# Weights converted quarter by quarter, and six blocks passed over each quarter

## The chip, the cores and the metric

The kernel runs on one core of a Trainium2 chip. The metric is the time of one execution on the device in microseconds (us). In the text TensorE is also PE, VectorE DVE, ScalarE ACT, GpSimd POOL and SyncE SP; PEld is TensorE's weight load.

## The reference

Two stages. A recurrent attention (RWKV-5) over 4 batches, 8 heads, 768 steps and head size 48, then a dense layer with a nonlinear step, on 3072 tokens of 384 numbers:

```
for t in range(S):
    cur = einsum('bhd,bhe->bhde', u * k[t], v[t])
    y[t] = einsum('bhd,bhde->bhe', r[t], state + cur)
    state = w * state + einsum('bhd,bhe->bhde', k[t], v[t])
x = y as (4*768, 384)
h = x @ w_in            # w_in  384 x 2048
g = h - tanh(h)
out = g @ w_out         # w_out 2048 x 384
```

The attention's inputs are 4-byte floats. The two weight matrices reach the kernel as 8-byte floats, which no engine computes with: the kernel loads them as pairs of 4-byte words and builds a 4-byte float from the bits.

## The kernel before, in words

**Attention.** The work is cut into 24 units. A unit takes 64 steps of two batches, all heads, so 128 tokens. It loads r, k and v (six transfers of 96 KB on SP's queue), scales k by powers of the decay (`kw`), turns r and k on TensorE into the PSUM tile `x_ps`, scales the turned r (`rT`) on VectorE and copies the turned k (`kT`) on ScalarE, multiplies them into `x_ps` again, applies the causal mask to the result with a predicated copy on VectorE (L390, into `at`), and multiplies `at` by v, and r by the running state, into the PSUM tile `yk_ps`. ScalarE copies the result into `xt`, six small transfers move the rest of the rows (`xt<-rest`, L410), and VectorE and GpSimd bring the state up to date (L416, L419). `rk` (L370, L371) and `du` (L374) give the diagonal, which GpSimd spreads into `at` (L376). Both PSUM tiles have one buffer, and each of the two batch pairs has one state, so a unit needs the one two before it.

**Dense.** Two units make a block, 12 blocks in all. A block goes over its 16 hidden tiles of 128 in 8 pairs (f, f+1). For a pair, twelve matmul instructions write `h` (L151); ScalarE makes s = h squared, th = tanh(h) and two squares q1, q2; GpSimd makes the mask `small` of the places where s is below 0.25 (L166); VectorE makes g = h - th, and, where h is small, replaces it by a polynomial `cube` (L167 to L171). Two pairs later eight matmul instructions add g times w_out into two PSUM tiles `o` (L177), which hold the sums of the whole block; then ScalarE copies them and SP writes them out (L190, L194).

**Weights.** `weight_steps` cuts them into 28 chunks, of 128 x 512 for w_in and 128 x 384 for w_out. Each is loaded on ScalarE's queue into a staging tile `st`, with two buffers, and converted in one step on ScalarE (L113), five on VectorE (L114 to L118) and two on GpSimd (L119, L120).

**Order.** Each engine takes its instructions in the order of the program. Python generators yield pieces of work, and `weave` interleaves them in proportion; a scheduler then orders the instructions by readiness, within what the buffers allow. `drive` weaves block 0 with the first half of the chunks, block 1 with the second half, and from then on the dense work of block j with the attention of block j+2. A dense block needs all 28 chunks, up to the last of its pairs.

Next to `near` stands `anywhere`, a second way for other decay values. It is in the program behind a branch on `flag` and isn't executed with these inputs.

Of the kernel before, what the change touches and what calls it, by code (L numbers as in the profile page):

```python
# [1 line left out]

# [6 lines left out]
F32 = mybir.dt.float32  # L9
# [10 lines left out]
SMALL = 0.25  # L20
# [13 lines left out]
L = 2  # L34

# [51 lines left out]
def weight_steps(nc, stage, w_in_sb, w_out_sb, moe_w_in, moe_w_out, d):  # L87
    V, A, G = nc.vector, nc.scalar, nc.gpsimd
    w_out_v = moe_w_out.rearrange("(ko ki) f -> ki ko f", ki=128)

    def weight(dst, pieces, dtype, cols):

        if dtype == F32:
            def g():
                for to, src in pieces:
                    nc.scalar.dma_start(out=dst[to], in_=src)

            return g


        assert dtype == I64

        def f():
            st = stage.tile([128, 512], I64, name="st", tag="st")[:, :cols]
            for to, src in pieces:
                nc.scalar.dma_start(out=st[to], in_=src)
            words = st.bitcast(U32).rearrange("p (n t) -> p n t", t=2)
            lo, hi = words[:, :, 0], words[:, :, 1]
            lo_f = st.bitcast(F32).rearrange("p (n t) -> p n t", t=2)[:, :, 0]
            part = stage.tile([128, 512], U32, name="part", tag="part")[:, :cols]  # L110
            part_f = part.bitcast(F32)
            bits = dst.bitcast(U32)
            A.activation(lo_f, lo, AF.Copy, scale=2.0**-52)  # L113
            V.tensor_scalar(part, hi, 3, 0x3FFFFFFF, ALU.logical_shift_left, ALU.bitwise_and)  # L114
            V.scalar_tensor_tensor(bits, hi, 0xC0000000, part, ALU.bitwise_and, ALU.bitwise_or)  # L115
            V.tensor_scalar(hi, hi, 20, 0x7FF, ALU.logical_shift_right, ALU.bitwise_and)  # L116
            V.scalar_tensor_tensor(dst, hi, 897.0, dst, ALU.is_ge, ALU.mult)  # L117
            V.tensor_scalar(part, bits, 0xFF800000, None, ALU.bitwise_and)  # L118
            G.tensor_tensor(part_f, part_f, lo_f, ALU.mult)  # L119
            G.tensor_tensor(dst, dst, part_f, ALU.add)  # L120

        return f

    weights = []
    for q in range(d.DFF // 512):
        sl = slice(q * 512, (q + 1) * 512)
        for ko in range(d.NK):
            pieces = []
            for to, kk, row, n in row_blocks(d):
                if kk is None:  # L130
                    row += ko * 2 * d.D
                if kk in (None, ko):
                    pieces.append((slice(to, to + n), moe_w_in[row : row + n, sl]))
            weights.append(weight(w_in_sb[:, ko, sl], pieces, moe_w_in.dtype, 512))
        for f in range(4 * q, 4 * q + 4):
            weights.append(weight(w_out_sb[:, f, :], [(slice(0, 128), w_out_v[:, f, :])], moe_w_out.dtype, d.DM))
    return weights


def make_dense(nc, work, gpool, ps_d, w_in_sb, w_out_sb, m1b, m2b, out, d, rows):  # L140

    V, A, T, G = nc.vector, nc.scalar, nc.tensor, nc.gpsimd

    def dense(j, xt):
        outs = [ps_d.tile([128, d.DM], F32, name=f"o{i}", tag=f"o{i}", bufs=1) for i in range(L)]

        def first(f):
            h = ps_d.tile([128, 2, d.NT], F32, name="h", tag="h")
            for z in range(2):
                for kk in range(d.NK):  # L150
                    T.matmul(h[:, z], w_in_sb[:, kk, (f + z) * 128 : (f + z + 1) * 128],  # L151
# [545 lines left out]
```

## Time and profile before

| | |
|---|---|
| Median of 3 runs | 727.84 us (726.28 to 729.05) |
| Profiled execution, its own time | 725.77 us |
| Span in the profile, first to last instruction | 724.0 us |
| Busy: PE, DVE, ACT, POOL | 620.9, 492.4, 279.5, 352.6 us |
| Mean granted TensorE clock | 0.946 |
| Transferred | 33.8 MB, mean 47 GB/s |

The profile's page divides the span into 40 slices of 18.1 us and gives each engine's busy share in tenths. A view by stage gives busy time in chosen stretches. Groups of instructions have a line, an engine, an operation, shapes and a count, then busy time in us and mean in ns, then the idle time just before them and what ended it. Timeline rows start with the start and the length in us. Waits are written "who <- whom: us in total, times, longest". PE's share of busy time is an average over two stages of different kinds, so the stretches are read apart.

### The profile page before, as it was taken

The numbers are of one execution on the slowest core, as the hardware profiler recorded it, in microseconds if no ns is written. First come the engines' busy times: TensorE is split into PE (matmuls) and PEld (weight loads), VectorE is DVE, ScalarE is ACT, GpSimd is POOL, SyncE is SP. The second block draws the span as 40 slices with busy tenths as digits, with TensorE's granted clock in tenths as the row PEclk, the third lists the DMA queues.
The fourth block names the chain that finished last, engine by engine and source line by source line (L and its number), as shares of the span: only waits on it lengthen the run. The fifth ranks groups of instructions, "written<-read, shape, count | busy, mean of one in ns | idle before, by whom it ended". The sixth has DMA issues, their size and how long they took to land.

```text
span 724.0 us, 13305 instructions
## 1 busy us (share of the span) xinstructions
PE 620.9 (86%) x5060; PEld 453.2 (63%) x5060; DVE 492.4 (68%) x739; ACT 279.5 (39%) x510; POOL 352.6 (49%) x289
## 2 busy tenths in 40 slices
PE   1462473657999999999999999999999999999996
PEld 0351452435776777777677777767777777777773
DVE  7764788989875664864865766748648656576563
ACT  1110413223443543444444434435435444354442
POOL 4775876758654543634545445436345243133231
PEclk9997586767999999999999999999999999999999
DMA  9457243422210211202102102112120010000001
GB/s 145 99 127 138 68 101 90 108 80 74 51 36 11 55 29 41 41 15 58 26 13 58 36 10 58 30 31 42 24 47 15 1 27 3 4 23 1 23 1 27
DMA packets 89722, 33.80 MB, mean 47 GB/s; under 512 B 80561, under 2 KB 86066, under 8 KB 89650
## 3 DMA queue, kind: packets, MB, share of 16 engines
q1 hardware_dynamic: 85042, 20.28, 14.9%
q10 hardware_dynamic: 4608, 12.59, 6.3%
q8 instruction: 42, 0.69, 0.4%
q14 instruction: 30, 0.25, 0.1%
HBM read 26.94 MB, written 4.72 MB: 44 GB/s over the span
## 4 chain that ended last, share of the span: by engine, by line
PE 68%; DVE 12%; DMA 8%; POOL 6%; issue 4%; SPq 1%; ACT 0%; ACTq 0%; DVEq 0%; POOLq 0%
PE o L177 33%; PE h L151 27%; PE yk_ps L348 4%; DMA st<-in_moe_w_out_dram 4%; DMA rt<-in_r_dram 3%; POOL part L119 3%; PE x_ps L363 2%; POOL rk L370 2%; POOL rk L371 2%; DVE st L116 1%; DVE part L114 1%; DVE w_in_sb L117 1%; DVE part L118 1%; DVE w_in_sb L115 1%; DVE cube L170 1%
## 5 line engine op out<-in xcount | busy, mean ns | idle before, releaser
L151 PE MATMUL h<-xt,w_in_sb 128*128 128x256 f32 x1152 | 276.4, 389 | 20.6 <-POOL w_in_sb L120 20.5
L177 PE MATMUL o<-w_out_sb,g 128*128 128x384 f32 x768 | 270.0, 498 | 11.8 <-DVE g L171 11.8
L166 POOL TENSOR_SCALAR small<-s 128x512 f32<-128x512 f32 x96 | 146.1, 1523 | 258.0 <-ACT s L162 249.7
L151 PEld LDWEIGHTS h<-xt,w_in_sb 128*128 128x128 f32 x1152 | 217.1, 194 | 59.8 <-POOL w_in_sb L120 22.9
L177 PEld LDWEIGHTS o<-w_out_sb,g 128*128 128x128 f32 x768 | 146.8, 194 | 102.4 <-issue 11.6
L167 DVE SCALAR_TENSOR_TENSOR cube<-s,h 128x512 f32<-128x512 f32 x96 | 65.7, 685 | 122.6 <-ACT th L163 122.4
L162 ACT ACTIVATE s<-h 128x512 f32<-128x512 f32 x96 | 57.3, 597 | 190.7 <-PE h L151 87.1
L170 DVE SCALAR_TENSOR_TENSOR cube<-q,cube 128x512 f32<-128x512 f32 x96 | 79.2, 825 | 7.6
L171 DVE COPY_PREDICATED g<-small,cube 128x512 f32<-128x512 int32 x96 | 78.5, 818 | 5.6
L169 DVE SCALAR_TENSOR_TENSOR cube<-q,cube 128x512 f32<-128x512 f32 x96 | 74.8, 779 | 0.0
L164 ACT ACTIVATE q<-s,m1b 128x512 f32<-128x512 f32 x96 | 69.3, 722 | 9.9 <-POOL part L119 9.9
L165 ACT ACTIVATE q<-s,m2b 128x512 f32<-128x512 f32 x96 | 69.0, 719 | 0.0
L168 DVE TENSOR_TENSOR g<-h,th 128x512 f32<-128x512 f32 x96 | 65.5, 682 | 0.0
L163 ACT ACTIVATE th<-h 128x512 f32<-128x512 f32 x96 | 56.8, 592 | 2.7 <-POOL part L119 2.7
L119 POOL TENSOR_TENSOR part<-part,st 128x384 f32<-128x384 f32 (+1 forms) x28 | 35.9, 1280 | 39.6 <-DVE part L118 22.8
L348 PE MATMUL yk_ps<-rT,state 48*64 48x64 f32 x704 | 27.7, 234 | 24.3 <-DVE state L416 19.3
L113 ACT ACTIVATE st<-st 128x384 f32<-128x384 uint32 (+1 forms) x28 | 17.1, 610 | 73.3 <-POOL part L119 34.5
L348 PEld LDWEIGHTS yk_ps<-rT,state 48*64 48x64 f32 x704 | 24.6, 146 | 33.1 <-issue 28.2
L376 POOL TENSOR_TENSOR at<-same,du 128x512 f32<-128x512 f32 x24 | 30.9, 1286 | 23.9 <-PE yk_ps L348 21.4
L365 DVE TENSOR_TENSOR rT<-x_ps,w_up 128x512 f32<-128x512 f32 x24 | 16.4, 685 | 29.3 <-PE x_ps L363 29.3
L374 DVE TENSOR_REDUCE du<-rk 128x8 f32<-128x384 f32 x24 | 13.2, 550 | 33.3 <-POOL rk L371 33.3
L370 POOL TENSOR_TENSOR rk<-rt,kt 128x384 f32<-128x384 f32 x24 | 26.6, 1109 | 16.5 <-DMA rt<-in_r_dram 9.5
(71 smaller groups left out, 459.8 us busy)
## 6 DMA issues: line engine op xcount, KB each, us to landing
st<-in_moe_w_out_dram ACTq DMA_DIRECT2D x16, 384.0 KB, 3.0
st<-in_moe_w_in_dram ACTq DMA_DIRECT2D x24, 192.0 KB, 3.3
rt<-in_r_dram SPq DMA_DIRECT2D x48, 96.0 KB, 3.1
kt<-in_k_dram SPq DMA_DIRECT2D x48, 96.0 KB, 3.0
vt<-in_v_dram SPq DMA_DIRECT2D x48, 96.0 KB, 2.8
out_dram<-o SPq DMA_DIRECT2D x48, 96.0 KB, 2.2
xt<-rest SPq DMA_DIRECT2D x144, 8.0 KB, 1.8
st<-in_moe_w_in_dram ACTq DMA_DIRECT2D x24, 64.0 KB, 3.3
```

Source lines behind the costliest of these rows:

```text
L119: G.tensor_tensor(part_f, part_f, lo_f, ALU.mult)
L151: T.matmul(h[:, z], w_in_sb[:, kk, (f + z) * 128 : (f + z + 1) * 128], xt[:, kk].rearrange("p b t -> p (b t)"), start=kk == 0, stop=kk == ...
L164: A.activation(q1, s, AF.Square, bias=m1b)
L165: A.activation(q2, s, AF.Square, bias=m2b)
L166: G.tensor_scalar(small, s, SMALL, None, ALU.is_lt)
L167: V.scalar_tensor_tensor(cube, s, C4, hf, ALU.mult, ALU.mult)
L168: V.tensor_tensor(gf, hf, th, ALU.subtract)
L169: V.scalar_tensor_tensor(cube, q1, K1, cube, ALU.add, ALU.mult)
L170: V.scalar_tensor_tensor(cube, q2, K2, cube, ALU.add, ALU.mult)
L171: V.copy_predicated(gf, small.bitcast(I32), cube)
L177: T.matmul(outs[i], g[:, z, i * C : (i + 1) * C], w_out_sb[:, f + z, :], start=f + z == 0, stop=f + z == d.NF - 1)
L348: tc.keep_in_program_order(T.matmul(*args, skip_group_check=True, **how))
```

## The change

- **Order of the dense work.** `FIRST = 6`. The hidden tiles are cut into four quarters of four (two pairs). After the attention of blocks 0 and 1, blocks 0 to 5 are taken over quarter 0, one after the other, then over quarter 1, 2 and 3. Beside quarter 0 run the twelve units of blocks 2 to 7. Blocks 6 to 11 run as before, each whole, with the attention of block j+2 beside it.
- **Partial sums.** After a quarter a block's sums leave PSUM: by a ScalarE copy into `part` for quarter 0 (L209), and by a VectorE addition for the others (L203). There are 12 `part` tiles and 8 `xt` tiles.
- **Weights.** Eight pieces, alternately a quarter of w_in and a quarter of w_out, each 128 x 1536. A piece is loaded by eight transfers (w_in) or one (w_out), into one of two staging buffers; the load of piece n+2 is issued after piece n is converted. Conversion has two steps on ScalarE (L142, L144) and five on VectorE (L141, L143, L146, L147, L149), none on GpSimd.
- **Attention of blocks 0 to 7.** `kw`, and the two products of `rk`, are on VectorE; the diagonal is spread by eight ScalarE instructions on 64 columns (L428). From block 8 on they are on GpSimd as before. The small `xt<-rest` transfers are made once per block, not per unit.
- **Mask.** `small` is made on ScalarE as relu(0.25 - s) (L181); a place counts where that is not zero. `cube` shares the buffer of `th`.
- The check of the decay uses a column sum on TensorE, and some set-up tiles share buffers.

The core of the diff:

```diff
+FIRST = 6
-            G.tensor_tensor(part_f, part_f, lo_f, ALU.mult)
-            G.tensor_tensor(dst, dst, part_f, ALU.add)
+        V.tensor_scalar(power, hi, 0x7FF00000, None, ALU.bitwise_and)
+        A.activation(power, power, AF.Relu, scale=8.0, bias=self.bias)
+        V.tensor_scalar(bits, hi, 0xFFFFF, 0x100000, ALU.bitwise_and, ALU.bitwise_or)
+        A.activation(lo_f, lo, AF.Copy, scale=2.0**-52)
+        yield
+        V.scalar_tensor_tensor(dst, bits, 2.0**-20, lo_f, ALU.mult, ALU.add)
+        V.scalar_tensor_tensor(power, hi, 0x80000000, power, ALU.bitwise_and, ALU.bitwise_or)
+        yield
+        V.tensor_tensor(dst, dst, power.bitcast(F32), ALU.mult)
...
-            G.tensor_scalar(small, s, SMALL, None, ALU.is_lt)
+        A.activation(small, s, AF.Relu, bias=smallb, scale=-1.0)
...
+        begun, whole = fs[0] > 0, fs[1] == d.NF
+        for i in range(L):
+            if begun:
+                o = sums.pop((j, i)) if whole else sums[j, i]
+                V.tensor_tensor(o, outs[i], o, ALU.add)
+            else:
...
+                    o = sums[j, i] = work.tile([128, d.DM], F32, name="part", tag="part", bufs=L * FIRST)
+                A.copy(o, outs[i])
...
+        weave(blocks([0, 1]), pieces([0, 1]))
+        after()
+        part = d.NF // 4
+        for q in range(4):
+            fs = (q * part, (q + 1) * part)
+            js = range(FIRST)
+            streams = [(chain.from_iterable(dense(j, xts[j], fs) for j in js), FIRST * part // 2)]
+            if q == 0:
+                streams.append(blocks(range(2, FIRST + 2)))
+            if q < 3:
+                streams.append(pieces([2 * q + 2, 2 * q + 3]))
+            weave(*streams)
...
+        early = n < L * (FIRST + 2)
+        E = V if early else G
+        E.tensor_tensor(kw[:, :, :D], kt, w_down, ALU.mult)
...
+        for h in range(H if early else 0):
+            A.mul(at[:, h % 2, h // 2], same, du[:, h : h + 1])
```

What the change moves, at the three places on which the prediction rests. First VectorE right after the set-up (`same`), where the first unit and the first weights meet. Before (`part` and `st` belong to the weights, `du`, `rT` and `at` to attention):

```order
L300 TENSOR_TENSOR same<-ident 128x64
L114 TENSOR_SCALAR part<-st 128x512
L115 SCALAR_TENSOR_TENSOR w_in_sb<-st,part 128x512
L374 TENSOR_REDUCE du<-rk 128x8
L116 TENSOR_SCALAR st<-st 128x512
L117 SCALAR_TENSOR_TENSOR w_in_sb<-st,w_in_sb 128x512
L118 TENSOR_SCALAR part<-w_in_sb 128x512
L365 TENSOR_TENSOR rT<-x_ps,w_up 128x512
```

Now, with the two first pieces and the third unit's `rk` ahead of the first unit's `kw` and `rT`:

```order
L141 TENSOR_SCALAR power<-st 128x1536
L143 TENSOR_SCALAR w_in_sb<-st 128x3x512
L421 TENSOR_TENSOR rk<-rt_156,kt 128x384
L422 TENSOR_TENSOR rk<-rk,ub 128x384
L143 TENSOR_SCALAR w_out_sb<-st 128x1536
L410 TENSOR_TENSOR kw_150<-kt,w_down 128x8x48
L416 TENSOR_TENSOR rT<-x_ps,w_up 128x512
```

One chunk of 512 columns stood ahead of the first `rT`; now both pieces of the first quarter do, and three units' loads.

Second, TensorE beside quarter 0: one unit (turns into `x_ps`, state and mask products, `at` times v) with the dense work between (`h` L165, `o` L195), now:

```order
L414 MATMUL x_ps<-ident,rt_156 128x128 x4
L165 MATMUL h<-xt,w_in_sb 128x256 x2
L414 MATMUL x_ps<-ident,kw_151 128x128 x4
L165 MATMUL h<-xt,w_in_sb 128x256
L396 MATMUL yk_ps<-rT,state_167 64x64 x16
L396 MATMUL x_ps<-rT,kT 64x64 x16
L165 MATMUL h<-xt,w_in_sb 128x256 x3
L195 MATMUL o_1553<-w_out_sb,g 128x384
L195 MATMUL o_1554<-w_out_sb,g 128x384
L396 MATMUL yk_ps<-at,vt_162 64x64 x16
L396 MATMUL yk_ps<-vt_162,kw_151 64x48 x16
```

Before, four pairs stood beside a unit in the later blocks; here it is one pair, and its matmuls fill the places where the unit waits for VectorE and ScalarE.

Third, VectorE in quarter 1 (of the change), where the last output-weight piece is first read (the second L143 piece of the order, into `w_out_sb`); its load stands in ScalarE's queue behind the activations that feed the L184 shown here:

```order
L184 SCALAR_TENSOR_TENSOR th<-q_2371,th 128x512
L149 TENSOR_TENSOR w_out_sb<-w_out_sb,power 128x1536
L185 SCALAR_TENSOR_TENSOR th<-q_2372,th 128x512
L141 TENSOR_SCALAR power<-st 128x1536
L186 COPY_PREDICATED g<-small,th 128x512
L182 TENSOR_TENSOR g<-h,th 128x512
L143 TENSOR_SCALAR w_out_sb<-st 128x1536
L183 SCALAR_TENSOR_TENSOR th<-s,h 128x512
```

All conversion of the last pieces has moved into quarter 1, between the five dense steps of a pair; before, no conversion stood beside blocks later than the second.

More of the change, by code (lines that the diff above doesn't have):

```diff
@@ L216, in drive, with blocks, pieces, steps @@
[L216 to L220 removed]
+    def blocks(js):
+        return chain.from_iterable(block(j) for j in js), nstep * L * len(js)
+    def pieces(ns):
+        def steps(n):
+            yield from weights.convert(n)
+            if n + 2 < weights.count:
+                weights.load(n + 2)
+        return chain.from_iterable(steps(n) for n in ns), 3 * len(ns)
@@ L420, in unit @@
         yield
-    drive(d, work, unit, dense, fetch, weights, 5)
+    drive(d, work, unit, dense, finish, fetch, weights, 5, after)
 @with_exitstack
```

290 lines of the change are left out of this document (150 added, 140 removed).

## The prediction

> **What bounds the kernel now.** I read the page's slices first, then busy time by stage, then waits of the early stage, then one period of the late stage.
>
> ```profile
> span 724.0 us, 13305 instructions
> PE   1462473657999999999999999999999999999996
> PEclk9997586767999999999999999999999999999999
> ```
> Each slice is 18.1 us. TensorE is full from the eleventh slice on; before it is half empty and its granted clock is low. The same by stage (us, then busy time of PE, PEld, DVE, ACT and POOL, granted clock, DMA share, GB/s):
>
> ```profile
> 60.00:180.00 120.00, 61.37 (x529) 43.70 (x530) 100.20 (x149) 33.58 (x63) 83.12 (x65) 0.70 0.36 91
> 200.00:600.00 400.00, 397.07 (x3428) 291.00 (x3427) 262.12 (x383) 174.96 (x320) 182.74 (x140) 1.00 0.16 32
> ```
> From 200 to 600 us PE is busy 397 of 400 us: that stage can only lose work, not waits. From 60 to 180 us VectorE is busy 100 of 120 us and GpSimd 83. The waits of that stage say what holds PE:
>
> ```profile
> ACT st L113 <- POOL part L119: 34.5, 6, 7.8
> PE h L151 <- POOL w_in_sb L120: 20.5, 6, 4.8
> PE yk_ps L348 <- DVE state L416: 19.3, 1, 19.3
> ```
> PE waits for weights whose last conversion step is on GpSimd, and ScalarE for buffers that GpSimd frees. So the first 200 us are conversion; the rest is PE's own work. How much of that work is done by 200 us (groups of 0 to 200, then of 200 to the end, then of 250 to 600; an L171 is one pair of hidden tiles, an L390 one attention unit, 96 and 24 in all):
>
> ```profile
> L171 DVE COPY_PREDICATED g<-small,cube 128x512 f32<-128x512 int32 x10 | 8.9, 890 | 0.1
> L390 DVE COPY_PREDICATED at<-before,x_ps 128x512 f32<-128x512 int32 x7 | 5.0, 720 | 4.2 <-POOL kw L359 2.2 <-PE x_ps L348 2.0
> ...
> L171 DVE COPY_PREDICATED g<-small,cube 128x512 f32<-128x512 int32 x86 | 69.6, 809 | 5.5
> L390 DVE COPY_PREDICATED at<-before,x_ps 128x512 f32<-128x512 int32 x17 | 12.3, 722 | 0.0
> ...
> L171 DVE COPY_PREDICATED g<-small,cube 128x512 f32<-128x512 int32 x56 | 46.1, 824 | 3.3
> L390 DVE COPY_PREDICATED at<-before,x_ps 128x512 f32<-128x512 int32 x14 | 10.1, 722 | 0.0
> ```
> Ten pairs and seven units in 200 us. The price of a pair, from the end, where no attention runs:
>
> ```profile
> 693.60 2.74 PE L177 MATMUL o<-w_out_sb,g 128*128 128x384 f32 x8
> 694.97 0.69 DVE L167 SCALAR_TENSOR_TENSOR cube<-s,h 128x512 f32<-128x512 f32 x1 [1.65 <-ACT th L163]
> 695.57 0.68 DVE L168 TENSOR_TENSOR g<-h,th 128x512 f32<-128x512 f32 x1
> 696.17 0.68 DVE L169 SCALAR_TENSOR_TENSOR cube<-q,cube 128x512 f32<-128x512 f32 x1
> 696.96 0.69 DVE L170 SCALAR_TENSOR_TENSOR cube<-q,cube 128x512 f32<-128x512 f32 x1
> 697.75 0.73 DVE L171 COPY_PREDICATED g<-small,cube 128x512 f32<-128x512 int32 x1
> 698.77 2.74 PE L177 MATMUL o<-w_out_sb,g 128*128 128x384 f32 x8
> ```
> Start to start 5.17 us per pair on PE at full clock, and 3.5 us of VectorE. A unit then costs PE (350 - 56 x 5.17) / 14 = 4.3 us. Check: after 200 us, 86 x 5.17 + 17 x 4.3 = 518 of 524 us; the other 6 us are the tail (last sums, copy and output).
>
> **The change, part by part.** I split the changed kernel into a start (until the first dense work on VectorE), pass 0 (six blocks on the first quarter, with twelve attention units), pass 1, and the rest.
>
> *Start.* It needs two weight pieces of 1.57 MB and, ahead of them in VectorE's queue, the loads of three units (1.77 MB). The transfers of the first 60 us:
>
> ```profile
> q1 hardware_dynamic: 18461, 3.56, 41.4%
> q10 hardware_dynamic: 1492, 4.11, 26.4%
> ```
> Of 16 engines x 60 us = 960 engine-us, q1 (small rows of r, k, v) takes 112 per MB and q10 (weights) 62 per MB. 1.77 x 112 + 3.15 x 62 = 393, over 16 engines 24.6 us; with issue and landing I take 28 us. Then VectorE has 42 instructions ahead of the first dense one: 33 small ones of about 0.6 us, and nine on 1536 columns. Their price from smaller ones:
>
> ```profile
> 69.23 0.42 DVE L114 TENSOR_SCALAR part<-st 128x512 uint32<-128x512 uint32 x1
> 69.68 0.69 DVE L115 SCALAR_TENSOR_TENSOR w_in_sb<-st,part 128x512 uint32<-128x512 uint32 x1
> 92.06 0.36 DVE L114 TENSOR_SCALAR part<-st 128x384 uint32<-128x384 uint32 x1 [1.18 <-DMA st<-in_moe_w_out_dram]
> 92.60 0.55 DVE L115 SCALAR_TENSOR_TENSOR w_out_sb<-st,part 128x384 uint32<-128x384 uint32 x1
> ```
> From 384 to 512 columns one source grows by 0.06 us and two by 0.14; so 1536 columns cost about 0.9 and 1.8 us, and a piece (two of the first, three of the second) 7.2 us. Seven of before's chunks, with 5 steps each, made one quarter. Start: 28 + 33 x 0.6 + 3 x 0.9 + 6 x 1.8 = 61, and 3 us for the chain of units: **64 us**. Bounds: 55 (transfers hidden better) to 75.
>
> *Pass 0.* VectorE: 12 pairs x 3.5 = 42; fifteen conversion steps, 22; and the attention products, which it takes from GpSimd. Rows for a unit:
>
> ```profile
> L374 DVE TENSOR_REDUCE du<-rk 128x8 f32<-128x384 f32 x10 | 5.5, 546 | 16.5 <-POOL rk L371 16.5
> L365 DVE TENSOR_TENSOR rT<-x_ps,w_up 128x512 f32<-128x512 f32 x7 | 4.8, 679 | 0.0
> L416 DVE TENSOR_TENSOR state<-yk_ps,state 128x384 f32<-128x384 f32 x4 | 2.2, 546 | 0.0
> L404 ACT COPY xt<-yk_ps 128x384 f32<-128x384 f32 x7 | 3.3, 474 | 24.1 <-DMA st<-in_moe_w_out_dram 8.3 <-PE x_ps L363 7.7 <-POOL part L119 6.6
> L407 ACT COPY rest<-yk_ps 128x128 f32<-128x128 f32 x7 | 1.8, 263 | 0.0
> ```
> The three moved products (kw, rk twice) have L416's shape, so 0.55 us each; with du, rT, L390 and the state 4.15 us a unit, twelve units 50. Sum 114 us. PE: 12 x 5.17 + 11 x 4.3 = 109 us at full clock (the first of the twelve units is mostly in the start); at the 0.70 of the 60-to-180 stage 156. ScalarE: mask, twelve times about 0.6; eight scalings of 64 columns per unit, each below L407's 0.26 us unless the scale held per partition adds to it, so between 0 and 2.1, I take 2.0; with its other work some 90 us, beside 109 or more: hidden. Without that cover it would still be under VectorE's 114. The mask leaves GpSimd, where 1.5 us per pair bounded nothing; that gains nothing itself. Six xt transfers per block instead of twelve: SP's queue gets shorter, price zero, since no PE wait above names it.
>
> VectorE and PE are both near 110 us, feed each other step by step, and take work strictly in order, so neither is at 100%. Ends: 112 us (VectorE without a gap) and 156 us (PE at the old clock). I take PE's work at 0.82, between 0.70 and 1.00, since PE would now be busy about four fifths of the time instead of half: 109 / 0.82 = **133 us**, 12.1 us per unit. On top 3 us, because in the order the second output-weight piece is wanted fifteen VectorE rows after its buffer is freed, some 12 us, with unit loads beside it.
>
> On shared ports the rows come first: L115 on 512 columns took 0.69 us at 69.68 with GpSimd idle, while its mean in the first 200 us was 1.22 us.
>
> ```profile
> L115 DVE SCALAR_TENSOR_TENSOR w_in_sb<-st,part 128x512 uint32<-128x512 uint32 x12 | 14.7, 1221 | 0.3
> ```
> So I price VectorE by the uncontended rows, as GpSimd has only the state product left early on; with contention the conversion steps would cost up to twice, 22 us more. The Trainium skill, "GPSIMD Engine Reference", Specifications, says GpSimd shares its SBUF interfaces with VectorE when that runs a two-port mode or two SBUF inputs; by that rule too VectorE gets cheaper here, and the trace agrees.
>
> *Pass 1.* VectorE: 42 + 12 additions of partial sums x 0.55 + thirteen conversion steps, 19 = 67.6 us against PE's 62: 5.6 us. The last output-weight piece is issued on ScalarE's queue some six VectorE rows, 5 us, before it is wanted: 1.57 MB need 6 us at 62 engine-us per MB over 16 engines, and 3 us to issue and land; the input piece before it is issued in parts and its last part as late. I add 4.4 us for both, since PE can live a few us on finished tiles. Together **10 us** (0 to 25). In passes 2 and 3 VectorE has 49 us against 62, hidden; so are the later copies of partial sums.
>
> *The rest.* After pass 0, 84 pairs and 8 units: 84 x 5.17 + 8 x 4.3 + 6 = **475 us**, PE-bound as before.
>
> Sum: 64 + 133 + 3 + 10 + 475 = 685 us of span. The profiled execution took 725.77 us for a span of 724.0, and the median of the runs is 2.1 us above it: 685 + 1.8 + 2.1 = **689 us**.
>
> **The rivals.**
> *Tight pass 0.* If PE stays busy enough for the full clock, VectorE's 112 us set pass 0, and pass 1 hides its 10: 64 + 112 + 475 + 4 = 655 us. For it: the slice at 180 to 200 us reaches clock 0.94 once PE is full. Against it: every early unit is a chain over PE, VectorE and ScalarE.
>
> ```profile
> 180.00:200.00 20.00, 20.00 (x192) 14.46 (x191) 17.49 (x28) 9.06 (x17) 12.73 (x11) 0.94 0.23 48
> ```
> The Trainium skill, "TensorE: Matmul & The Clock Gate", Part 1, has the full clock released by about 3.4 us of sustained activity and lost after an idle window; by that rule pass 0 runs at full clock if its gaps stay short, which is this rival's 655 us.
>
> *A slow unit chain: slower.* The units' PSUM tile has one buffer, so a unit's turns cannot start before the previous unit's mask is applied. Early units came at this pace:
>
> ```profile
> 20.89 0.73 DVE L390 COPY_PREDICATED at<-before,x_ps 128x512 f32<-128x512 int32 x1 [2.16 <-POOL kw L359]
> 35.28 0.71 DVE L390 COPY_PREDICATED at<-before,x_ps 128x512 f32<-128x512 int32 x1
> 49.98 0.73 DVE L390 COPY_PREDICATED at<-before,x_ps 128x512 f32<-128x512 int32 x1 [2.02 <-PE x_ps L348]
> ```
> 14.5 us each, with no dense pair between. If half of a pair's 5.17 us falls into the chain, a unit takes 17 us: 64 + 11 x 17 = 251 instead of 197, in all 743 us. It decides from 15.6 us per unit. Against it: those 14.5 us hold conversion and contended GpSimd steps that are gone from a unit.
>
> *Exposed weights.* Two staging buffers hold two whole pieces, so a piece's load waits for the conversion two before. If all six later pieces expose 12 us (1.57 MB at 129 GB/s, the mean of the first 60 us) and not the 7 of my sum, 689 + 6 x 12 - 7 = 754 us. Against it: the order leaves four of the six loads 25 VectorE rows or more.
>
> *The order does not change.* Then about 728 us; the printed order speaks against it, with twelve pairs and sixteen units in front of the second quarter.
>
> **How the numbers follow.** Forecast 0.56, tight pass 0.22, slow chain 0.12, exposed weights 0.06, unchanged 0.04. Range 652 to 722: it takes in most of the tight case and the lighter half of the slow chain, and leaves out both ends above. What this kernel's runs tell from no change is about 0.5%, 724.2 to 731.5. Faster: 0.56 + 0.22 + half the slow chain's chance, 0.06 = 0.84; same: 0.06, from the unchanged case and part of the chain; slower 0.10.
>
> **What would show it.** Right: first dense VectorE work near 64 us; units' masks (L444 now) about 12 us apart up to some 200 us; PE full from there, with 5.17 us per pair; waits of PE on VectorE of some 10 us between 200 and 270 us. Wrong: units 15 us apart or more; PE idle on weight transfers for more than 20 us; a pair period above 5.2 us after pass 1, for then the extra additions or the mask on ScalarE cost what I put at nothing; or a clock of 1.0 through pass 0, which is the tight case.

## The result, and the profile after

The changed kernel takes 673.47 us (median of four runs, 671.99 to 676.01), the kernel before on the same chip 728.44. The ratio is 0.9252, with a 95% interval of 0.9214 to 0.929. The forecast was 689 us, with a range of 652 to 722. The profiled execution took 674.14 us. Of the executions reported below one is a slow one, of the four with the eight steps on VectorE (688.46 us); the other three have a median of 677.75 us.

The page of the changed kernel, with its 40 slices of 16.8 us:

```profile
span 672.3 us, 12904 instructions
PE   0047898898999999999999999999999999999995
PEclk9999799999999999999999999999999999999999
```

TensorE is at eight or nine tenths from the fifth slice on, where before it lay between one and seven tenths up to the tenth. By stage (us, then busy time of PE, PEld, DVE, ACT and POOL, granted clock, DMA share, GB/s), with the cuts at the first dense row of VectorE and at the end of the twelfth pair:

```profile
0.00:77.00 77.00, 30.61 (x515) 24.39 (x516) 44.55 (x75) 23.86 (x61) 7.37 (x23) 1.00 0.73 142
77.00:201.00 124.00, 112.82 (x1860) 83.36 (x1860) 100.45 (x152) 83.88 (x202) 23.20 (x23) 0.97 0.56 105
201.00:672.00 471.00, 463.11 (x2690) 339.18 (x2688) 346.73 (x496) 266.03 (x459) 30.70 (x28) 1.00 0.09 21
```

In the middle stretch PE is busy 113 of 124 us, at a clock of 0.97, and GpSimd only 23. Before, the stretch from 60 to 180 us had PE busy for half of the time, at 0.70. The rows of VectorE's timeline at which the stretches were cut, and the masks of attention units at both ends of quarter 0:

```profile
77.12 0.67 DVE L182 TENSOR_TENSOR g<-h,th 128x512 f32<-128x512 f32 x1
80.80 0.73 DVE L444 COPY_PREDICATED at<-before,x_ps 128x512 f32<-128x512 int32 x1 [1.55 <-PE x_ps L396]
187.37 0.71 DVE L444 COPY_PREDICATED at<-before,x_ps 128x512 f32<-128x512 int32 x1
200.02 0.73 DVE L186 COPY_PREDICATED g<-small,th 128x512 f32<-128x512 int32 x1
```

Eleven units lie between the two masks: (187.37 - 80.80) / 11 = 9.7 us each. Late in the program a pair still takes PE what it took before, 5.17 us from start to start:

```profile
644.18 2.75 PE L165 MATMUL h<-xt,w_in_sb 128*128 128x256 f32 x12
649.36 2.75 PE L165 MATMUL h<-xt,w_in_sb 128*128 128x256 f32 x12
```

So the gain lies in the first 200 us. By then the kernel before had done ten pairs and seven units, and the changed one twelve pairs and sixteen units. At 5.17 us a pair and 4.3 us a unit that is 2 x 5.17 + 9 x 4.3 = 49 us of PE work, of the 51.7 us by which the span got shorter. This is a count of work done early, worked out from these prices; it is not measured by itself.

### The profile page after: what moved, and what is told of

It is laid out like the page before. It is cut to its first block, busy times and chain, and to the rows that moved or that the text cites. A ratio compares the mean times of both kernels' runs of the same rounds, so it can differ in the third digit from the quotient of the medians.

```text
span 672.3 us, 12904 instructions
## 1 busy us (share of the span) xinstructions
PE 606.5 (90%) x5062; PEld 446.9 (66%) x5062; DVE 491.7 (73%) x721; ACT 373.8 (56%) x722; POOL 61.3 (9%) x73
## 4 chain that ended last, share of the span: by engine, by line
PE 68%; DVE 1%; issue 0%; ACT 0%; DVEq 0%
PE o L195 32%; PE h L165 32%; PE yk_ps L396 2%; PE x_ps L414 1%; PE x_ps L396 1%; DVE th L183 0%; DVE g L182 0%; DVE power L147 0%; DVE th L185 0%; DVE part L203 0%; DVE g L186 0%; ACT q L179 0%; DVE th L184 0%; ACT s L177 0%; DVE du L425 0%
## 5 line engine op out<-in xcount | busy, mean ns | idle before, releaser
L165 PE MATMUL h<-xt,w_in_sb 128*128 128x256 f32 x1152 | 274.4, 384 | 4.8 <-DMA xt<-rest 3.6
L195 PE MATMUL o<-w_out_sb,g 128*128 128x384 f32 x768 | 265.9, 488 | 1.1 <-DVE part L203 0.9
L165 PEld LDWEIGHTS h<-xt,w_in_sb 128*128 128x128 f32 x1152 | 215.8, 191 | 48.6 <-issue 3.7
L195 PEld LDWEIGHTS o<-w_out_sb,g 128*128 128x128 f32 x768 | 144.4, 190 | 82.4 <-DVE part L203 2.5
L186 DVE COPY_PREDICATED g<-small,th 128x512 f32<-128x512 int32 x96 | 75.5, 786 | 7.9
L185 DVE SCALAR_TENSOR_TENSOR th<-q,th 128x512 f32<-128x512 f32 x96 | 71.2, 742 | 6.5 <-DVE th L184 0.5
L184 DVE SCALAR_TENSOR_TENSOR th<-q,th 128x512 f32<-128x512 f32 x96 | 66.9, 697 | 6.5
L181 ACT ACTIVATE small<-s,smallb 128x512 f32<-128x512 f32 x96 | 68.9, 717 | 0.0
L183 DVE SCALAR_TENSOR_TENSOR th<-s,h 128x512 f32<-128x512 f32 x96 | 65.8, 685 | 2.5
L476 POOL TENSOR_TENSOR state<-state,power 128x384 f32<-128x384 f32 x22 | 21.5, 979 | 162.5 <-DVE state L473 102.3
L428 ACT ACTIVATE at<-same,du 128x64 f32<-128x64 f32 x128 | 33.3, 339 | 2.2 <-PE yk_ps L396 2.1
L418 ACT COPY kT<-x_ps 128x512 f32<-128x512 f32 x24 | 14.1, 585 | 35.0 <-PE x_ps L414 33.3
L414 PE MATMUL x_ps<-ident,kw 128*128 128x128 f32 x96 | 17.0, 305 | 16.5 <-DVE rT L416 16.4
L396 PEld LDWEIGHTS yk_ps<-at,vt 64*64 64x64 f32 x768 | 14.6, 144 | 22.7 <-issue 12.5
L396 PE MATMUL yk_ps<-at,vt 64*64 64x64 f32 x768 | 18.0, 236 | 11.4 <-issue 6.8
```

The costliest lines, as they stand in the source:

```text
L181: A.activation(small, s, AF.Relu, bias=smallb, scale=-1.0)
L183: V.scalar_tensor_tensor(cube, s, C4, hf, ALU.mult, ALU.mult)
L184: V.scalar_tensor_tensor(cube, q1, K1, cube, ALU.add, ALU.mult)
L185: V.scalar_tensor_tensor(cube, q2, K2, cube, ALU.add, ALU.mult)
L186: V.copy_predicated(gf, small.bitcast(I32), cube)
L195: T.matmul(outs[i], g[:, z, i * C : (i + 1) * C], w_out_sb[:, f + z, :], start=f + z == fs[0], stop=f + z == fs[1] - 1)
```

## Experiments

Most runs change the changed kernel in one respect, or carry one part of the change into the kernel before; where more is changed, the text says so. "Before" on the chips of these runs lay between 725.97 and 726.55 us, and on the chip of the changed kernel at 728.44. So a difference of 2 or 3 us between a run and the changed kernel's 673.47 us can be the chip's; the ratio compares on one chip.

### All of the change but the order

```diff
-FIRST = 6
+FIRST = 0
-        weave(blocks([0, 1]), pieces([0, 1]))
+        weave(blocks([0]), pieces([0, 1, 2, 3]))
+        weave(blocks([1]), pieces([4, 5, 6, 7]))
         after()
```

All blocks are then taken whole. Only the first four units have their early products on VectorE.

> All of the change but the order: eight pieces converted without GpSimd beside blocks 0 and 1, then whole blocks. Theory O (the order carries most of the gain, since dense work may start after one quarter): eight pieces cost VectorE 8 x 7.2 = 58 us and the transfers 12.6 MB x 62 + 2.4 MB x 112 over 16 engines = 65 us, so dense work starts at 105 to 125 us with PE nearly idle until then, and 96 x 5.17 + 20 x 4.3 + 6 = 588 us follow: 695 to 715 us. Theory G (relief of GpSimd carries most, the order little): below 685 us.

Measured: 703.63 us, ratio 0.9685 (0.9666 to 0.9704), as theory O had it; the first dense row of VectorE stands at 119.88 us. The two stretches from 100 us on:

```profile
100.00:140.00 40.00, 20.20 (x305) 16.45 (x306) 35.22 (x39) 24.28 (x41) 14.50 (x12) 0.65 0.30 76
140.00:180.00 40.00, 39.95 (x339) 29.70 (x339) 28.60 (x41) 21.04 (x38) 7.77 (x8) 1.00 0.12 24
```

PE is full from 140 us on, earlier than in the kernel before, but from 100 to 140 us it works half of the time, since a whole block needs all eight pieces, and there is no other dense work to do. The conversion and the other moves are worth 23 us without the order; the order adds 30 us to them.

### The order alone

```diff
-        A.activation(small, s, AF.Relu, bias=smallb, scale=-1.0)
+        nc.gpsimd.tensor_scalar(small, s, SMALL, None, ALU.is_lt)
-        early = n < L * (FIRST + 2)
+        early = False
-        V.scalar_tensor_tensor(power, hi, 0x80000000, power, ALU.bitwise_and, ALU.bitwise_or)
...
-        V.tensor_tensor(dst, dst, power.bitcast(F32), ALU.mult)
+        G.tensor_tensor(part_f, part_f, lo_f, ALU.mult)
+        G.tensor_tensor(dst, dst, part_f, ALU.add)
```

Mask, early products and the eight conversion steps of before, on the pieces of 1536 columns and in the new order. The pieces, three or four times as long as the chunks of before, come with the order in this run, so it is the order together with long GpSimd steps.

> The order alone: mask, early products and the last two conversion steps are back on GpSimd, with before's eight conversion steps on 1536 columns. Theory O: at most 695 us, since GpSimd's early work (8 pieces x 2 x 3.9 us, 16 units x 4.6 us, 12 masks x 1.5 us, 154 us) still fits into the first 200 us. Theory G: 710 us or more, GpSimd being the bound of the first 200 us again.

Measured: 742.39 us, ratio 1.0231 (1.0211 to 1.025): slower than before, on the side of theory G. A stretch of it, the waits of VectorE on GpSimd (total, times, longest) and its first and last unit mask of the front:

```profile
140.00:180.00 40.00, 29.82 (x408) 20.42 (x412) 32.17 (x29) 10.64 (x21) 36.25 (x19) 0.83 0.52 87
...
DVE du L427 <- POOL rk L424: 22.9, 9, 6.3
...
52.87 0.72 DVE L446 COPY_PREDICATED at<-before,x_ps 128x512 f32<-128x512 int32 x1
...
257.32 0.73 DVE L446 COPY_PREDICATED at<-before,x_ps 128x512 f32<-128x512 int32 x1 [0.39 <-PE x_ps L398]
```

GpSimd is busy 36 of 40 us, and fifteen units take 13.6 us each, up to 257 us. The order asks for sixteen units in the front instead of seven, and as long as a unit takes this long, that costs more than the early dense work brings. What shorter GpSimd steps would make of this order was not run. So neither half carries the gain: the order alone loses 16 us, the rest alone gains 23, and both together gain 55.

### The mask alone, in the kernel before

```diff
-            G.tensor_scalar(small, s, SMALL, None, ALU.is_lt)
+            A.activation(small, s, AF.Relu, bias=smallb, scale=-1.0)
```

> The kernel before with the mask alone moved to ScalarE as relu(0.25 - s). Theory (before's front end is bound by the conversion, whose GpSimd steps hold VectorE, and a pair's mask is only 1.5 us on an engine that has 83 of 120 us busy there): GpSimd gets 10 x 1.5 = 15 us less work in the first 200 us, of which a few us reach the end: 720 to 727 us. Rival (the mask's turn in GpSimd's queue is what the units' chain waits for also in before, as it is 7 us in the changed kernel): 715 us or less. Third: ScalarE, which starts the chain of a dense pair, is lengthened by 0.5 us a pair: 728 to 733.

Measured: 720.25 us, ratio 0.9904 (0.9867 to 0.9941), about 7 us, as the first theory had it.

```profile
60.00:180.00 120.00, 62.22 (x541) 43.36 (x541) 98.96 (x154) 38.48 (x71) 70.02 (x59) 0.73 0.37 93
```

GpSimd is busy 70 us in this stretch instead of 83, PE 62 instead of 61: most of the freed 13 us isn't used there. That fits a pace set by the conversion, which this run leaves as it was.

### One part taken back at a time

Three runs put one part of the change back on GpSimd and leave the rest. First the mask:

```diff
-        A.activation(small, s, AF.Relu, bias=smallb, scale=-1.0)
+        nc.gpsimd.tensor_scalar(small, s, SMALL, None, ALU.is_lt)
```

> The mask alone back on GpSimd. Theory O: 0 to 4 us slower than the changed kernel's 673.5, because PE is full after 200 us and GpSimd nearly idle before. Theory G: 8 us slower or more.

Measured: 680.63 us, ratio 0.9381 (0.9356 to 0.9406), 7 us more than the changed kernel, between the two forecasts and nearer to theory G. A unit takes 10.8 us instead of 9.7.

Then the early products and the diagonal:

```diff
-        early = n < L * (FIRST + 2)
+        early = False
```

> The early products and the spread diagonal back on GpSimd. Theory O: within 6 us of 673.5 either way, for VectorE gets 1.65 us per unit less and ScalarE 2.7 us less, while a unit's chain gets GpSimd's 1.1 us products. Theory G: 15 us slower or more.

Measured: 691.54 us, ratio 0.952 (0.9466 to 0.9574), 18 us more, as theory G had it. A unit takes 12.05 us, and VectorE waits for GpSimd's `rk`:

```profile
DVE du L425 <- POOL rk L422: 21.2, 7, 6.7
```

Then the conversion, with before's eight steps on the pieces of 1536 columns, the last two on GpSimd:

```diff
-        V.scalar_tensor_tensor(power, hi, 0x80000000, power, ALU.bitwise_and, ALU.bitwise_or)
...
-        V.tensor_tensor(dst, dst, power.bitcast(F32), ALU.mult)
+        G.tensor_tensor(part_f, part_f, lo_f, ALU.mult)
+        G.tensor_tensor(dst, dst, part_f, ALU.add)
```

> Conversion alone back to before's steps, the last two on GpSimd, on pieces of 1536 columns; mask and products stay as changed. Theory C (the front's length is the pace of the attention units, which steps of GpSimd stretch when a unit or VectorE has to wait for them; the mask cost 7 us and the products 18): the state product of every unit now queues behind conversion steps of about 3.9 us and two-input steps on VectorE slow down, so a unit takes 10.5 to 12 us and the time is 685 to 705 us. Theory B (only GpSimd's busy sum counts, and 62 us more fit into 200): 673 to 680 us.

Measured: 720.83 us, ratio 0.9921 (0.9897 to 0.9946), 47 us more: with this part alone taken back, nearly all of the gain is gone. Both forecasts were too low. Theory C had the pace right, but not what follows from it: a unit takes 12.1 us (the fifth and sixteenth masks stand at 88.02 and 220.86 us), the same as in the run before, whose time is 29 us shorter. Against the changed kernel, 7 us are lost before the fifth mask, 26 between the two, and 15 behind the sixteenth, where pieces are still converted. A reason stands in the timeline, where GpSimd's and VectorE's rows overlap (start, length):

```profile
96.45 0.68 DVE L186 SCALAR_TENSOR_TENSOR th<-q,th 128x512 f32<-128x512 f32 x1
96.50 4.00 POOL L150 TENSOR_TENSOR power<-power,st 128x1536 f32<-128x1536 f32 x1 [1.45 <-DMA kt<-in_k_dram]
97.06 0.72 DVE L446 COPY_PREDICATED at<-before,x_ps 128x512 f32<-128x512 int32 x1
97.67 3.38 DVE L187 SCALAR_TENSOR_TENSOR th<-q,th 128x512 f32<-128x512 f32 x1
100.58 3.75 POOL L151 TENSOR_TENSOR w_in_sb<-w_in_sb,power 128x1536 f32<-128x1536 f32 x1
100.98 3.77 DVE L424 TENSOR_TENSOR rk<-rk,ub 128x384 f32<-128x384 f32 x1
```

L187 takes 0.69 us otherwise. Here it starts while GpSimd's L150 runs, takes 3.38 us, and ends at 101.05, 0.55 us after L150. L424, 0.55 us otherwise, takes 3.77 us and ends 0.42 us after GpSimd's L151. L446 in between, one of whose inputs is in PSUM, takes its usual 0.72 us. So a VectorE instruction with two inputs in SBUF that starts beside such a GpSimd instruction isn't slowed in proportion; it waits for the end of it. The Trainium skill, "SBUF — State Buffer", Who interferes with whom, says this: a VectorE instruction with two SBUF inputs contends with a GpSimd instruction that reads SBUF, and whichever issues first keeps the shared ports for its whole length. The trace agrees, with 3.38 beside 4.00 us. Not every one of the sixteen GpSimd steps met such an instruction: in this trace twelve VectorE rows are held by them, for 0.4 to 3.2 us each, 29 us in all, and each ends 0.4 to 0.6 us after the GpSimd step.

### The eight steps, with GpSimd's two on VectorE

To tell GpSimd's share from that of the longer form, the same eight steps were run with the last two on VectorE.

```diff
-        part, part_f, G = power, power.bitcast(F32), self.nc.gpsimd
+        part, part_f, G = power, power.bitcast(F32), self.nc.vector
```

> The changed kernel with the eight conversion steps of before, as in the run that took 720.8 us, but the last two of them on VectorE instead of GpSimd: VectorE gets two more instructions of 1536 columns and two sources per piece, about 1.75 us each by the rows of those steps, GpSimd none. Theory (GpSimd's two-source instructions beside VectorE are what costs, whatever the form of the conversion): 3.5 us more VectorE work for each of the two pieces of the start and the two pieces beside quarter 0, half of it or more on the path, 680 to 690 us, 31 us or more below 720.8. Rival (the eight-step form itself costs: a longer chain per piece and a staging buffer freed later, so weights and units wait): 710 us or more.

Measured: 680.69 us, ratio 0.9369 (0.9311 to 0.9427), at the lower edge of the theory's range. 40 of the 47 us are gone (43 by the median of 677.75), so they come with GpSimd's two steps, and the form is worth some 4 to 7. From 64 to 230 us, first the changed kernel, then its conversion with GpSimd, then all eight steps on VectorE:

```profile
64.00:230.00 166.00, 151.62 (x2131) 112.08 (x2131) 140.55 (x205) 113.01 (x259) 26.15 (x24) 0.98 0.50 102
```

```profile
64.00:230.00 166.00, 133.50 (x2108) 99.42 (x2109) 131.04 (x171) 89.24 (x224) 57.15 (x33) 0.89 0.48 95
```

```profile
64.00:230.00 166.00, 146.53 (x2096) 108.18 (x2095) 152.56 (x206) 105.38 (x250) 32.95 (x24) 0.95 0.48 101
```

VectorE is busier in the third (153 us) than in the second (131 us), and yet PE does 13 us more there. A view of busy time alone would have chosen the second.

How much of the 40 us is held time can be summed from the rows: over the first 300 us, VectorE's rows are 36.3 us longer than the shortest of their own line, tile and shape in the run with GpSimd, 11.6 in the run with all steps on VectorE, and 7.0 in the changed kernel. So held rows make some 25 of the 40 us, if all of them delay the end. The other 15, among them units and staging buffers that wait for GpSimd's queue, were not told apart.

### GpSimd's steps in pieces

```diff
-        G.tensor_tensor(part_f, part_f, lo_f, ALU.mult)
-        G.tensor_tensor(dst, dst, part_f, ALU.add)
+        for k in range(dst.shape[1]):
+            G.tensor_tensor(part_f[:, k], part_f[:, k], lo_f[:, k], ALU.mult)
+        for k in range(dst.shape[1]):
+            G.tensor_tensor(dst[:, k], dst[:, k], part_f[:, k], ALU.add)
```

> The changed kernel with the conversion of before on its quarter pieces (eight steps, the last two on GpSimd), but each of the two GpSimd steps cut into three instructions of 512 columns (four of 384 for w_out) instead of one of 1536. With whole GpSimd instructions it took 720.8 us, 47 us more than the changed kernel, and VectorE instructions with two SBUF inputs took 3.4 to 3.8 us where a 3.6 us GpSimd instruction ran. Theory (such a VectorE instruction is held until the GpSimd instruction that runs beside it ends): in pieces the GpSimd instructions last about 1.2 us, and what VectorE waits at one of them falls from about 3 to about 1 us; VectorE rows of two SBUF inputs between 1 and 2 us, none above 2.2, and the time falls by a half to two thirds of the 47 us, to 690 to 700 us. Rival (the two engines share a port evenly, so the same bytes take the same time however they are cut): VectorE's mean durations stay near those of the whole instructions, and the time stays within 5 us of 721.

Measured: 711.2 us, ratio 0.9776 (0.9732 to 0.982). Neither forecast holds: 10 of the 47 us come back, not 21 to 31, and not under 5.

```profile
95.44 5.08 POOL L151 TENSOR_TENSOR power<-power,st 128x512 f32<-128x512 f32 x3 [0.94 <-DMA kt<-in_k_dram]
95.91 1.77 DVE L188 SCALAR_TENSOR_TENSOR th<-q,th 128x512 f32<-128x512 f32 x1
98.22 1.16 DVE L189 SCALAR_TENSOR_TENSOR th<-q,th 128x512 f32<-128x512 f32 x1
99.30 1.65 DVE L426 TENSOR_TENSOR rk<-rk,ub 128x384 f32<-128x384 f32 x1
100.49 4.79 POOL L153 TENSOR_TENSOR w_in_sb<-w_in_sb,power 128x512 f32<-128x512 f32 x3
100.86 1.78 DVE L190 COPY_PREDICATED g<-small,th 128x512 f32<-128x512 int32 x1
```

The lengths are those of the theory: a held instruction takes 1.2 to 1.8 us instead of 3.4 to 3.8. But three pieces take GpSimd 5.08 and 4.79 us where the whole took 4.00 and 3.75, and five VectorE instructions meet them here (those shown, and a product `kw` at 103.14 us that takes 1.01) instead of two. That reads as the two engines taking turns: cutting shortens the single wait, and leaves much of the sum of both engines' work, which go one after the other. The theory was right on the single wait and wrong to count the time by it. Summed as above, VectorE's rows are 27.5 us too long instead of 36.3: the pieces take 9 us off the held time, and the run is 10 us shorter.

### What sets the start

Four runs bear on the first 77 us. First, the w_in piece in four transfers instead of eight, because their issue took ScalarE's queue some 19 us:

```diff
-        for to, kk, row, rows in row_blocks(d):
-            if kk is None:
...
+        for i in range(2):
+            src = w_in[: d.NK * 2 * d.D, sl].rearrange("(k r) f -> r k f", k=d.NK)[i * d.D : (i + 1) * d.D]
+            parts.append((slice(i * PAD, i * PAD + d.D), slice(0, d.NK), src))
+            row = (2 * d.NK + i) * d.D
+            src = w_in[row : row + d.D, sl].rearrange("(k x) f -> x k f", k=d.NK)
+            parts.append((slice(i * PAD + d.D, (i + 1) * PAD), slice(0, d.NK), src))
```

> A quarter of w_in is loaded by four transfers instead of eight; the bytes are the same. If the start (first dense step on VectorE at 77 us, 64 predicted) is late because ScalarE issues the eight loads over 18.8 us, each waiting for an earlier transfer, the first piece lands 5 us earlier or more and the time falls to 664 to 670 us. If unit loads or the chain of units set the start, 671 to 676 us.

Measured: 676.35 us, ratio 0.931 (0.927 to 0.9349), not faster than the changed kernel, and the fifth unit's mask at 80.86 instead of 80.80 us. The first issues end 7 us earlier (at 12.3 instead of 19.6 us), and VectorE still reads the piece first at 23.06 instead of 22.95. The issue of these loads doesn't set the start.

Then four first blocks instead of six:

```diff
-FIRST = 6
+FIRST = 4
```

> Four blocks in the passes instead of six. Theory C: four units leave the front (4 x 9.7 = 39 us) and come back in the full stage with four pairs (4 x 4 + 4 x 5.17 = 37 us), so the front alone changes nothing; but the conversion of the last pieces meets shorter passes, VectorE 51 us against PE's 41 in pass 1: 673 to 685 us. If it is the number of pairs at hand that fills PE early, it is slower still, above 685 us.

Measured: 674.65 us, ratio 0.93 (0.9273 to 0.9326), 1 us more by the medians and 3 to 4 by the ratios, within theory C's range. The number of first blocks is not what the gain hangs on, from four to six.

Then the diagonal by one VectorE product instead of eight ScalarE instructions:

```diff
-        for h in range(H if early else 0):
-            A.mul(at[:, h % 2, h // 2], same, du[:, h : h + 1])
-        if not early:
-            G.tensor_tensor(at, same[:, None, None, :].to_broadcast([128, 2, NP, SHORT]),
+        if True:
+            E.tensor_tensor(at, same[:, None, None, :].to_broadcast([128, 2, NP, SHORT]),
```

> The diagonal of an early unit is spread by one VectorE product of 512 columns (0.69 us) instead of eight ScalarE instructions (8 x 0.34 = 2.7 us). If VectorE's busy time paces the units, 12 x 0.7 = 8 us slower, 679 to 684 us. If ScalarE stands in the chain of a unit, faster, 660 to 671 us. If neither, within 2 us of 673.5.

Measured: 667.2 us, ratio 0.92 (0.9173 to 0.9226), 6 us faster than the changed kernel by the medians and 4 by the ratios, whose intervals touch, and the fastest run: ScalarE stood in the chain. ScalarE's group in the changed kernel, then the stretch from 28 to 64 us of the changed kernel:

```profile
L428 ACT ACTIVATE at<-same,du 128x64 f32<-128x64 f32 x128 | 33.3, 339 | 2.2 <-PE yk_ps L396 2.1
...
28.00:64.00 36.00, 17.58 (x343) 14.21 (x344) 21.56 (x29) 11.44 (x26) 1.69 (x2) 1.00 0.58 102
```

and the same stretch with one VectorE product, with its first dense row and its masks of the same two units as above:

```profile
28.00:64.00 36.00, 22.97 (x402) 19.18 (x406) 29.60 (x39) 9.21 (x15) 4.54 (x3) 1.00 0.63 114
...
68.38 0.67 DVE L182 TENSOR_TENSOR g<-h,th 128x512 f32<-128x512 f32 x1
...
73.51 0.72 DVE L442 COPY_PREDICATED at<-before,x_ps 128x512 f32<-128x512 int32 x1
...
180.62 0.73 DVE L442 COPY_PREDICATED at<-before,x_ps 128x512 f32<-128x512 int32 x1
```

Eight times 0.339 us, 2.7 us a unit, stood in the chain of a unit. In the start, where little dense work hides it, that made the first dense row 8.7 us later (77.12 against 68.38), the fifth mask 7.3 us later (80.80 against 73.51), and the eleventh after it 6.8 us later. Between the two masks the units take 9.7 us in both kernels. So VectorE's extra 0.7 us a unit doesn't show in the pace, and ScalarE's 2.7 us cost only in the start.

Last, this version with the loads of attention three units ahead, and five first blocks to make room for the buffers:

```diff
+NEAR = 3
-FIRST = 6
+FIRST = 5
-        fetch(1)
+        for n in range(1, NEAR):
+            fetch(n)
-    load = ctx.enter_context(tc.tile_pool(name="n_load", bufs=3))
+    load = ctx.enter_context(tc.tile_pool(name="n_load", bufs=NEAR + 1))
-        if n + AHEAD < d.NU:
-            fetch(n + AHEAD)
+        if n + NEAR < d.NU:
+            fetch(n + NEAR)
```

> The changed kernel with the diagonal spread by one VectorE product (that alone gave 667.2 us), the loads of attention issued three units ahead instead of two, and, to make room for the buffers, five first blocks instead of six (four instead of six made 1 us in the changed kernel). Theory L (the start is late because VectorE waits for the units' own loads, three to five us at a time, behind the small rows of r, k and v): the waits on rt and kt in the first 70 us fall by 8 us or more, the first predicated copy of a pair comes near 66 instead of 74 us, and the time is 658 to 662 us. Rival D (the DMA engines set the start: a third unit's load ahead of the weights only moves the wait to the weights): the first predicated copy at 72 us or later, and 666 to 672 us.

Measured: 682.56 us, ratio 0.9396 (0.9362 to 0.9429), 15 us slower than without it. Neither forecast had that. Its waits for k in the first 100 us:

```profile
DVE rk L423 <- DMA kt<-in_k_dram: 4.7, 2, 3.0
```

The waits on loads are still there, so more depth doesn't take them away, and the fifth mask came at 85.56 instead of 73.51 us: 12 of the 15 us are lost by then. What makes it slower, the loads or the order that comes out with five blocks, was not told apart, since two things were changed at once. With four blocks alone the fifth mask came at 79.07 instead of 80.80 us, which speaks for the loads.

## Why the prediction was right, step by step

The time fell into the range, 15 us below the forecast, and the place and mechanism were as predicted: the front end, not the rest. Three terms of the sum were off, and two of them cancel, which is luck.

**Start: 64 predicted, 77 measured.** The step that failed is the "3 us for the chain of units", together with ScalarE's scalings, which were put under "hidden" for pass 0 and stand nowhere in the start. The last of the first loads, of output weights, is read at 31.64 us, where the sum had 28. From there VectorE is busy 32.7 us, which is the 33 us of its 42 instructions, and idle 12.8 us instead of 3. VectorE waits for loads, and for the units' turns through PE, time and again before the first dense row; three of these waits, and the row at 31.64:

```profile
30.57 0.56 DVE L421 TENSOR_TENSOR rk<-rt,kt 128x384 f32<-128x384 f32 x1 [5.00 <-issue]
31.64 0.95 DVE L143 TENSOR_SCALAR w_out_sb<-st 128x1536 uint32<-128x1536 uint32 x1
48.32 0.56 DVE L421 TENSOR_TENSOR rk<-rt,kt 128x384 f32<-128x384 f32 x1 [3.03 <-DMA kt<-in_k_dram]
59.19 0.56 DVE L421 TENSOR_TENSOR rk<-rt,kt 128x384 f32<-128x384 f32 x1 [4.13 <-DMA rt<-in_r_dram]
```

In the first 77 us VectorE is busy 44.6 us and idle 32.5. The scalings were bounded by 2.1 us a unit and taken at 2.0; they are 2.7 us, and the run with one product instead shows that they weren't hidden there. There the same weight row stands at 29.24 us and VectorE idles 6.4 us from it to the first dense row, so 8.7 of the 13 us are gone. The other 4 were not traced to one cause; the four-transfer run shows only that it isn't the issue of the weights. One price was off as well, and small: an input-weight piece's L143 writes 128x3x512 and takes 1.75 us, not 0.9.

**Pass 0: 136 predicted, 124 measured.** The 109 us of PE work stood, with 112.8 us busy. The mis-sized term is the clock, taken at 0.82, between the old stage's 0.70 and 1.00; it was 0.97:

```profile
64.00:100.00 36.00, 33.07 (x510) 25.73 (x511) 32.91 (x48) 27.10 (x72) 4.75 (x4) 0.91 0.55 118
100.00:140.00 40.00, 35.80 (x707) 26.14 (x706) 31.62 (x53) 25.58 (x69) 3.89 (x4) 1.00 0.56 99
```

PE is busy nine tenths of the time, and it has the full clock from 100 us on. In the clock the rival "tight pass 0" was the better reading. The rule of the Trainium skill's page "TensorE: Matmul & The Clock Gate", Part 1, cited with it, agrees with the second of these rows: from 100 to 197 us PE is never idle for more than 1.34 us. It does not show why the clock is 0.66 from 75 to 85 us, since PE had idled for at most 1.23 us in the 14 us before. But that rival's bound of 112 us by VectorE (114 by the prediction's own sum) is not what set the pass: VectorE was busy 100 of 124 us, PE 113. Its 655 us were missed by the late start and PE's remaining 11 us idle. A unit took 9.7 us, not 12.1.

**Pass 1: 10 predicted, 1 measured.** The one wait of PE's matmuls on VectorE that the profile lists after 200 us is 0.9 us long, and the last output weights came in time, issued on ScalarE's queue and read by VectorE 7.6 us later, without a wait:

```profile
PE o L195 <- DVE part L203: 0.9, 1, 0.9
...
216.01 0.39 ACTq L125 DMA_DIRECT2D st<-in_moe_w_out_dram  x1
...
223.62 0.94 DVE L143 TENSOR_SCALAR w_out_sb<-st 128x1536 uint32<-128x1536 uint32 x1
```

The failed step is that VectorE's excess of 5.6 us in this pass, and a late piece, would reach PE. VectorE is indeed full from 201 to 263 us, busy 61.1 of 62 us, and PE 60.9. The excess runs on into the next 62 us, where VectorE has only 47.9 us to do. The prediction granted PE a few us on finished tiles for the late piece, and none for the excess.

**The rest: 475 predicted, 471.5 measured,** from 200.8 us to the end, with the same period per pair. The mask on ScalarE and the additions of partial sums cost nothing there, as predicted.

Together: 77.1 + 123.7 + 471.5 = 672.3 us of span, against 64 + 136 + 10 + 475 = 685. The start's +13 and pass 0's -12 cancel; what is left is pass 1 and the rest, -13.

**The rivals.** The slow unit chain was not met, since it decides from 15.6 us per unit, and a unit took 9.7. But a chain of units can pace the front: with the order alone a unit takes 13.6 us, the front ends at 257 us, where the rival had put it at 251, and the time is 742 us. That these lie so near to the rival's 251 and 743 is chance: the rival counts eleven units of 17 us from 64 us on, and the run has eleven of 13.6 us from its fifth mask at 108.01. What keeps the changed kernel off it is the removal of GpSimd's work. The prediction said that these steps "are gone from a unit" in half a sentence; the runs show that the sign hangs on it. Exposed weights did not appear, and the order did change.

**Contention.** The prediction took VectorE's rows without contention and allowed 22 us for it in the conversion steps only. For the changed kernel that was right: its held rows sum to 7.0 us over 300 us. As the price of contention it was too small and too narrow: where the two conversion steps stay on GpSimd, VectorE instructions with two SBUF inputs are held, attention's and the pairs' too, and the run takes 40 us more.

## What to carry to other kernels

An order that pulls work forward pays only if the chain that feeds it is fast enough: measure the pace of that chain, here one attention unit, and multiply it by the number of turns that the new order puts in front. The pace is not all: two runs here had units of 12.1 us and times 29 us apart. When VectorE and GpSimd both have work with two SBUF inputs, expect a time nearer to the sum of the two than to the larger; moving a step to an idle GpSimd can cost more than the step takes on a busy VectorE. Parts of a change that need each other can't be priced one at a time: here they cost 47, 30, 18 and 7 us when each is taken back, in sum almost twice the gain.

## What the runs showed of the hardware that was not expected

- The wait of a VectorE instruction with two SBUF inputs runs to the end of GpSimd's instruction, with 0.42 to 0.55 us after it: 0.69 us becomes 3.38, and 0.55 becomes 3.77. An instruction with one input from PSUM isn't held: L184, g = h - th with h in PSUM, takes at most 0.71 us in the first 300 us of that run, nine of its 23 rows beside GpSimd.
- The wait goes the other way as well. GpSimd's mask took 1.52 us in the mean in the kernel before. In the run with only the mask taken back its median is 1.49 us, but seventeen of the 96 take 1.6 to 3.9 us, all beside VectorE's work in the first 263 us. One of them took 2.73 us, with VectorE's row beside it at its usual length:

```profile
L166 POOL TENSOR_SCALAR small<-s 128x512 f32<-128x512 f32 x96 | 146.1, 1523 | 258.0 <-ACT s L162 249.7
```

```profile
148.76 2.73 POOL L181 TENSOR_SCALAR small<-s 128x512 f32<-128x512 f32 x1 [9.73 <-ACT s L177]
149.13 0.55 DVE L410 TENSOR_TENSOR kw<-kt,w_down 128x384 f32<-128x384 f32 x1
```

- The granted clock doesn't follow PE's busy share over 40 us. Two neighbouring stretches of the kernel with GpSimd's steps in pieces have the same share and a clock of 0.99 and 0.80:

```profile
140.00:180.00 40.00, 30.88 (x478) 22.34 (x477) 32.73 (x43) 24.88 (x62) 20.92 (x17) 0.99 0.47 105
180.00:220.00 40.00, 30.52 (x457) 23.34 (x458) 26.43 (x36) 14.05 (x38) 11.61 (x12) 0.80 0.46 77
```

So a clock estimated from the busy share of a long stretch, as the prediction did, is only a guess. Cut finer, the low clock stands right behind two idle stretches of PE, of 5.22 us (up to 181.58) and 6.68 us (up to 211.74): it is 0.50 from 182 to 186 us and from 212 to 220, and 1.00 from 186 to 205. That is not the whole rule, since the 0.66 of the changed kernel from 75 to 85 us has no such stretch before it; no run changed the idle time alone.

- The clock of 1.00 that the profile gives for the first 60 us of the changed kernel isn't borne out by its matmuls: those of `x_ps<-ident,kw` (L414) take 435 ns in the mean from 20 to 58 us, and 285 ns from 100 to 180.
